# One two-column size matmul, one layer-1 score partial, staged sums and paired weight-block instructions in a TensorE-bound transformer kernel

## The chip, the cores and the metric

The kernel runs on one core of one Trainium2 chip. The metric is the device time of one execution in microseconds (us). Most executions of one kernel agree within 0.3%. "PE" is TensorE, "DVE" VectorE, "ACT" ScalarE, "POOL" GpSimd, "SPq" the queue from which most transfers are issued.

## The reference

Two identical layers work on x of 2048 tokens by 1024, with the same weights in both layers:

```python
def _A_ref(x, wqkv, wo):                 # H = 32 heads of 32; each token sees W = 8 keys, 2 apart
    qkv = (x @ wqkv) ...                 # cut: split into q, k, v and heads
    logits = einsum("bhsd,bhswd->bhsw", q, kg) * Dh ** -0.5   # kg: the 8 gathered keys
    attn = softmax(where(mask, logits, -1e9))
    return einsum("bhsw,bhswd->bhsd", attn, vg) ... @ wo

def _B_ref(x, w1, w3, w2):               # F = 3584
    return (silu(x @ w1) * (x @ w3)) @ w2

x = x + _A_ref(_layernorm(x), wqkv, wo)
x = x + _B_ref(_layernorm(x), w1, w3, w2)
x = x + _A_ref(_layernorm(x), wqkv, wo)
x = x + _B_ref(_layernorm(x), w1, w3, w2)
```

## The kernel before

The tokens are worked in units of 512: four units in layer 0, four in layer 1. In the first two units the gate, up and w2 matmuls are done plainly. While they run, the kernel prepares the same weights for a seven-product (Strassen-Winograd) multiplication, which the other six units use. Preparing a group of weights is a chain across engines:

1. ScalarE squares and sums the group; one small matmul against ones adds the sums over partitions (the "size"); VectorE turns the size into a power-of-two scale.
2. ScalarE copies the four corners of the group, scaled, into a block buffer; VectorE makes the three other blocks as differences; GpSimd issues the stores to DRAM (`t_d`). There are two block buffers, so copies wait for earlier stores.
3. The w2 blocks are made in the same two buffers, after those of w1 and w3. Only when ScalarE has copied w2 is its weight buffer released, and the K and V weights of layer 1 are loaded into released buffers. The second half of the Q weights takes a buffer that the last w3 copies release (in the kernel before it is issued at 495.3, when they end).

The parts that matter here:

```python
def pe_requests(limit=1, must=False):      # small matmuls asked for by the other engines
    act_background()
    while pe_queue and limit and (must or pe_queue[0][0]() + 3.5 <= now["pe"]):
        pe_queue.pop(0)[1]()
        limit -= 1

def act_background():                      # ScalarE's optional work
    for queue in (acts, sizes, parts, reads):
        while True:
            s = head(queue)
            if s is None or max(now["act"], s[1]) + s[0] > now["pe"] + 2.2:
                break
            take_act(queue)

def weight_size(m, g, w, at, got):
    ...                                    # cut: two Square activations into size[:, m, g, 0:2]
    def scale_item(ps, r):
        def emit():
            scale_of(ps[:], up, down)
            got["at"] = now["dve"] + 0.1
        yield 0.8, r, emit
    def add_up(t):
        ps = side.tile([P, 1], FP32, name="size", tag="sd")
        for i in range(2):
            nc.tensor.matmul(ps[:], lhsT=ones[:], rhs=size[:, m, g, i:i + 1], start=i == 0, stop=i == 1)
        makes.append([scale_item(ps, pe(2, t)), None])
    t = now["act"] + 2.5
    pe_queue.append((lambda: t, lambda: add_up(t)))

def weight_sums(m, g, w, got):
    ...                                    # cut: waits for the size and for a free buffer
        for i, (kh, fh) in ((0, (0, 0)), (1, (0, 1)), (3, (1, 0)), (5, (1, 1))):
            yield 0.61, max(got["at"], stored[a]), lambda: nc.scalar.activation(
                b[:, i], w[:, kh * KQ:(kh + 1) * KQ, c0:c0 + P], ACTF.Copy,
                scale=up_scale[:, m, g:g + 1])
        makes.append([differences(m, g, a, now["act"] + 0.1), None])

def differences(m, g, a, r):
    for out, x, y in ((4, 5, 1), (1, 1, 0), (2, 5, 1), (6, 3, 2)):
        yield 0.46, r, lambda: nc.vector.tensor_tensor(b[:, out], b[:, x], b[:, y], op=ALU.subtract)
    ...                                    # cut: two GpSimd stores to t_d
```

A pattern runs through all of it. Every instruction is emitted by a list scheduler written in Python. `now` holds a modelled clock for each engine; each `yield` tells the scheduler a duration (0.61, 0.46, 0.8 ...), the time at which the input is ready, and what to emit. The gate `now["pe"] + 2.2` and the `+ 3.5` decide, by these modelled clocks, whether an instruction goes in here or later. The engines execute in the emitted order.

The activation sums for the seven products (`norm_sums`) are four VectorE instructions, which wait for the transposed activations. The attention scores of one half are products on VectorE, folded down to two partials in `psm`; eight matmuls (`gather_heads`) add these over the head dimension.

Of the kernel before, what the change touches and what calls it, by code (L numbers as in the profile page):

```python
# [17 lines left out]
def kernel(  # L18
# [136 lines left out]

    def bank(name):
        if name == "po":
            return side.tile([P, 512], FP32, name=name, tag="sd")
        return psum.tile([P, 512], FP32, name=name, tag="mm")
# [48 lines left out]
    size2 = const.tile([P, 16], FP32, name="size2")  # L208
    total = const.tile([P, 1], FP32, name="total")
# [4 lines left out]
    h16 = hT[:].bitcast(FP16)  # L214
    t2_d = [dram.tile([P, 7, (b - a) // 2, 512], FP16, name=f"t2_d{i}") for i, (a, b) in enumerate(fsplits)]
    t_d = [[dram.tile([P, 14, KT // 2, P], FP16, name=f"t_d{m}_{g}") for g in range(NG)] for m in range(2)]
    qkv_d = [[dram.tile([P, KT, S], BF16, name=f"qkv_d{l}_{i}") for i in range(3)] for l in range(2)]
# [56 lines left out]
    sums_of, sums_free = {}, [False]  # L274

    def norm_sums(key):

        while not sums_free[0]:
            yield "blocked"
        sums_free[0] = False  # L280
        xnT = xnTs[key]
        KQ = KT // 2
        a11, a12, a21, a22 = [xnT[:, k0:k0 + KQ, t0:t0 + HT] for t0 in (0, HT) for k0 in (0, KQ)]
        s1, s2, s4 = sums[:, 0], sums[:, 1], sums[:, 2]

        def step(out, x, y, op):
            return 0.62, xnT_at[key], lambda: nc.vector.tensor_tensor(out, x, y, op=op)

        yield step(s1, a21, a22, ALU.add)
        yield step(s2, s1, a11, ALU.subtract)  # L290
        yield step(a21, a11, a21, ALU.subtract)
        yield step(s4, a12, s2, ALU.subtract)
        sums_of[key] = now["dve"] + 0.1
# [60 lines left out]

    def act_background():
        for queue in (acts, sizes, parts, reads):
            while True:
                s = head(queue)
                if s is None or max(now["act"], s[1]) + s[0] > now["pe"] + 2.2:
                    break  # L360
                take_act(queue)
# [206 lines left out]
    def score_steps():  # L568

        V = nc.vector  # L570
        for g, (l, h) in enumerate(halves):
# [13 lines left out]
            yield from tree(W, tree_bufs[0], mul_qk, lambda w_: psm[:, w_], True)  # L585
# [5 lines left out]
            def gather_heads(t):  # L591
                at["L"] = L = side.tile([P, W, BLK], FP32, name="L", tag="sd")
                for i in range(2):
                    for a in range(4):
                        nc.tensor.matmul(L[32 * a:32 * (a + 1), :, :], lhsT=gather[:],
                                         rhs=psm[:, :, i, a * BLK:(a + 1) * BLK], start=i == 0, stop=i == 1,
                                         skip_group_check=True)
                at["t"] = pe(3, t) + 0.2
# [71 lines left out]
    for u in range(len(units)):  # L670
        for f0, f1 in fsplits:
# [9 lines left out]
            if u >= TU:  # L681
                seq += [("t2", fsplits.index((f0, f1)), b, nq) for b in range(7)]
# [91 lines left out]

    def sum_later(key):
# [28 lines left out]
    def q_part(l, c, which, ws, then=()):  # L804
# [8 lines left out]
        for t0 in range(0, KT, SG):  # L813
# [19 lines left out]
            if l == 0:  # L833
                stored[:] = landed, landed
# [5 lines left out]
        qkv_at[l, c, which] = landed  # L840
        if which == 2:
# [12 lines left out]
    def weight_size(m, g, w, at, got):  # L854
# [8 lines left out]
        def scale_item(ps, r):  # L863
            def emit():
                scale_of(ps[:], up, down)
                got["at"] = now["dve"] + 0.1
            yield 0.8, r, emit

        def add_up(t):
            ps = side.tile([P, 1], FP32, name="size", tag="sd")  # L870
            for i in range(2):
                nc.tensor.matmul(ps[:], lhsT=ones[:], rhs=size[:, m, g, i:i + 1], start=i == 0, stop=i == 1)
            makes.append([scale_item(ps, pe(2, t)), None])
# [4 lines left out]
    def weight_sums(m, g, w, got):  # L878
# [4 lines left out]
        for a in range(2):  # L883
# [4 lines left out]
            for i, (kh, fh) in ((0, (0, 0)), (1, (0, 1)), (3, (1, 0)), (5, (1, 1))):  # L888
                c0 = fh * 256 + a * P
                yield 0.61, max(got["at"], stored[a]), lambda: nc.scalar.activation(  # L890
                    b[:, i], w[:, kh * KQ:(kh + 1) * KQ, c0:c0 + P], ACTF.Copy,
                    scale=up_scale[:, m, g:g + 1])
            makes.append([differences(m, g, a, now["act"] + 0.1), None])
        made.add((m, g))

    pending, stored, made, held = [0, 0], [0.0, 0.0], set(), []
    junk = hsum[:].bitcast(BF16).rearrange("p k t -> p (k t)")

    def differences(m, g, a, r):

        b = blocks[a]
        for out, x, y in ((4, 5, 1), (1, 1, 0), (2, 5, 1), (6, 3, 2)):
            yield 0.46, r, lambda: nc.vector.tensor_tensor(b[:, out], b[:, x], b[:, y], op=ALU.subtract)
        pending[a] -= 1
        nc.gpsimd.dma_start(t_d[m][g][:, 4 * a:4 * (a + 1)], b[:, 0:4])
        nc.gpsimd.dma_start(t_d[m][g][:, 8 + 3 * a:8 + 3 * (a + 1)], b[:, 4:7])
        stored[a] = now["dve"] + 7.0
# [24 lines left out]
    def measure2(i, n, at):  # L932

        w = hT[:, 0:n, :]
        for a, b in ((0, n // 2), (n // 2, n)):
            def square():
# [3 lines left out]
                if len(measured) == 16:  # L940
                    scales2()
# [15 lines left out]
    def scales2():  # L957

        def scale_item(ps, r):
            def emit():  # L960
                nc.vector.tensor_reduce(total[:], ps[:], op=ALU.add, axis=AX.X)
                scale_of(total[:], up2[:], down2[:])
                got2["at"] = now["dve"] + 0.1
            yield 1.1, r, emit

        def add_up(t):
            ps = side.tile([P, 16], FP32, name="size", tag="sd")
            nc.tensor.matmul(ps[:], lhsT=ones[:], rhs=size2[:], start=True, stop=True)
            makes.append([scale_item(ps, pe(1, t)), None])
# [6 lines left out]
    def sums_of_w2(i, f, ws, loaded):  # L976
# [6 lines left out]
        for j, (fh, hh) in ((0, (0, 0)), (2, (0, 1)), (1, (1, 0)), (5, (1, 1))):  # L983
# [4 lines left out]
        def rest():  # L988
            for out, x, y in ((4, 5, 2), (2, 2, 0), (3, 5, 2), (6, 1, 3)):
                yield 0.46, r, lambda: nc.vector.tensor_tensor(b[:, out], b[:, x], b[:, y], op=ALU.subtract)  # L990
# [17 lines left out]

    def products(u, f0, f1, hold):

        key = ("B", *units[u])
        xnT = xnTs[key]
        KQ = KT // 2
        sides = dict(P1=(0, xnT[:, 0:KQ, 0:HT]), P5=(1, sums[:, 0]), P6=(2, sums[:, 1]), P2=(3, xnT[:, KQ:KT, 0:HT]),
                     P7=(0, xnT[:, 0:KQ, HT:CH]), P3=(1, sums[:, 2]), P4=(2, xnT[:, KQ:KT, HT:CH]))
        groups = [dict(m=m, g=g0 // FG, f=g0 - f0) for g0 in range(f0, f1, FG) for m in range(2)]
# [97 lines left out]
        def acc():  # L1114
            return psum.tile([P, 2, HT], FP32, name="st", tag="mm")

        def run(G, name, out, start, ready=0.0):
            blk, rhs = sides[name]
            w = G["early"] if name in ("P1", "P5", "P6", "P2") else G["late"]
            for a in range(2):  # L1120
                for k in range(KQ):
                    nc.tensor.matmul(out[:, a, :], lhsT=w[:, a, blk, k, :], rhs=rhs[:, k, :],  # L1122
                                     start=start and a == 0 and k == 0, stop=k == KQ - 1, skip_group_check=True)
            return pe(4.05, max(ready, sums_of[key]))

        def consume(G, q, src, r):
            m, g, f = G["m"], G["g"], G["f"] + 2 * (q % 2)
            inv = down_scale[:, m, g:g + 1]
# [14 lines left out]
        def head_part(i, name):  # L1143
            G = groups[i]
            s5, su, s22 = snaps[i % 2], snaps[2], snaps[3]
            if name == "P1":
                G["early"] = weight("early")
                G["A"] = acc()
                r = run(G, name, G["A"], True)
                G["B"] = acc()  # L1150
                nc.scalar.copy(G["B"][:], G["A"][:])  # L1151
                G["tB"] = act(0.5, r)
            elif name == "P5":
                G["D"] = acc()
                r = run(G, name, G["D"], True)
                nc.scalar.activation(s5, G["D"][:], ACTF.Copy, scale=down_scale[:, G["m"], G["g"]:G["g"] + 1] if G["m"] else 1.0)
                G["t5"] = act(0.5, r)
            elif name == "P6":
                r = run(G, name, G["A"], False, G["tB"])
                nc.scalar.copy(su, G["A"][:])  # L1160
                G["tU"] = t = act(0.5, r)
                background(t + 0.8)
                nc.vector.tensor_tensor(G["D"][:], G["D"][:], su, op=ALU.add)  # L1163
                G["tD"] = dve(0.68, max(t, G["t5"])) + 0.1
            elif name == "P2":
                r = run(G, name, G["B"], False, G["tB"])
                release(1)
                consume(G, 0, G["B"][:], r)
            elif name == "P7":
                G["late"] = weight("late")  # L1170
                r = run(G, name, G["A"], False, G["tU"])
                background(r + 0.8)
                if G["m"]:
                    s22 = tight[:, 0]
                    nc.vector.scalar_tensor_tensor(s22, G["A"][:], down_scale[:, 1, G["g"]:G["g"] + 1], s5,
                                                   op0=ALU.mult, op1=ALU.add)
                else:
                    nc.vector.tensor_tensor(s22, G["A"][:], s5, op=ALU.add)  # L1178
                G["tC"] = dve(0.68, r) + 0.1
                consume(G, 3, s22, G["tC"])  # L1180
            elif name == "P3":
# [194 lines left out]
```

## Time and profile before

| | before |
|---|---|
| time, median of 3 (lowest to highest) | 1545.78 us (1545.72 to 1547.3) |
| span of the profiled execution | 1546.5 us |
| PE / DVE / ACT busy | 1529.9 / 1191.9 / 883.3 us |
| mean granted clock | 0.997 |

Two lines of the page of the kernel before, the span and the busy times of the engines with their share of the span:

```profile
span 1546.5 us, 25176 instructions
...
PE 1529.9 (99%) x9694; PEld 992.7 (64%) x9694; DVE 1191.9 (77%) x2048; ACT 883.3 (57%) x1388; POOL 158.8 (10%) x308
```

TensorE bounds the kernel: 1529.9 of 1546.5 us. But the share is of no use for judging what is left to gain. The Trainium skill ("Perfetto Trace Analysis", Identifying the Most-Contended Engine) says that the busy share of matmuls is a poor measure of headroom. A matmul at half clock counts as busy too (2.00 of 2.00 us at a clock of 0.50 in a stretch shown below). The lines to read are the waits and the granted clock.

The next lines are the largest of TensorE's waits in the kernel before: what waited, for which engine and line, the total in us, how many times, and the longest.

```profile
PE L L595 <- DVE psm L506: 4.1, 1, 4.1
PE w L1057 <- DVE hT L1028: 2.6, 3, 1.4
PE w L1057 <- ACT big L1077: 1.9, 4, 0.6
...
PE po L762 <- DVE x_sb L767: 0.9, 1, 0.9
```

The first is a single wait. The timeline of VectorE before that place shows its cause. The columns are start and length in us, then the instructions; in brackets stand the idle time before them and what ended it.

```profile
530.91 1.23 DVE L582 TENSOR_TENSOR tree<-qT,kT 128x2048 bf16<-128x2048 bf16 x1
542.21 0.69 DVE L287 TENSOR_TENSOR big<-xnT 128x1024 f16<-128x1024 f16 x1 [10.08 <-DMA xnT<-xn]
542.82 0.42 DVE L506 TENSOR_TENSOR psm<-tree 128x512 bf16<-128x512 bf16 x1
543.16 0.68 DVE L287 TENSOR_TENSOR big<-big,xnT 128x1024 f16<-128x1024 f16 x1
...
544.96 0.68 DVE L502 TENSOR_TENSOR tree<-tree 128x1024 bf16<-128x1024 bf16 x1
545.68 0.42 DVE L506 TENSOR_TENSOR psm<-tree 128x512 bf16<-128x512 bf16 x1
```

VectorE works in order. Activation sums (L287) had been put ahead of the folds (L502, L506), and the first waited 10.08 us for the transposed activations. So the last fold ended at 546.1. The timeline of TensorE:

```profile
537.83 4.26 PE L820 MATMUL ps<-xnT,wqkv 128*128 128x512 f16 x19
546.16 1.05 PE L595 MATMUL L<-psm,gather 128*32 128x512 bf16 x8 [4.06 <-DVE psm L506]
```

The gather waits 4.06 us for that fold. The windows view of the kernel before then shows the price in clock (length of the stretch; busy time and count of PE, PEld, DVE, ACT and POOL; granted clock; DMA share; GB/s):

```profile
546.00:548.00 2.00, 1.84 (x10) 0.52 (x10) 0.82 (x3) 0.00 (x0) 0.00 (x0) 0.50 1.01 418
...
550.00:552.00 2.00, 2.00 (x6) 0.82 (x5) 1.29 (x2) 1.22 (x3) 0.00 (x0) 0.50 1.16 313
```

The clock is 0.50 in these two stretches; the half clock runs from 545.2 to 552.0, 6.8 us. TensorE works in it only from 546.2 on, 5.8 us, of which half, 2.9 us, is lost. The stall costs 4.06 + 2.9 = 7.0 us. The Trainium skill ("TensorE: Matmul & The Clock Gate", Part 1: The HAM clock gate) has the half clock follow an idle window of about 3.4 us; this place agrees roughly, with 4.06 us idle, the clock halved 3.1 us after the wait began (542.1), and a stretch twice 3.4 us long.

The groups that the change rewrites, from the views of the kernel before by line and shape (count, busy us, mean ns, then idle time before):

```profile
L890 ACT ACTIVATE big<-w1t,up_scale 128x512 f16<-128x512 bf16 x56 | 36.1, 711 | 9.2 <-DVE psm L506 5.1 <-DMA t_d<-big 4.1
...
L903 DVE TENSOR_TENSOR big<-big 128x512 f16<-128x512 f16 x112 | 47.2, 423 | 15.9 <-ACT big L890 13.7
...
L595 PE MATMUL L<-psm,gather 128*32 128x512 bf16 x128 | 10.3, 399 | 4.1 <-DVE psm L506 4.1
...
L872 PE MATMUL size<-size,ones 128*128 128x1 f32 x56 | 7.0, 229 | 0.0
```

### The profile page before, as it was taken

To read this page: it belongs to the slowest core of one execution; us is meant where nothing else is said; L and a number is where in the kernel's file an instruction comes from. 1 tells how busy PE (TensorE), PEld (TensorE's weight loads), DVE (VectorE), ACT (ScalarE), POOL (GpSimd) and SP (SyncE) were. 2 spreads that over 40 slices of the span, in tenths; PEclk is the share of its full clock that TensorE was granted. 3 is DMA by queue.
4 is the path that set the end of the run, shared out by engine and by line. 5 is a ranking of instruction groups with operands and counts; after the bars stand their busy time and mean duration, and the time that the engine had idled before them with its cause. 6 is when DMAs were issued, how large, how long until landed. Compare 5 with 4: busy or idle time off the path is not lost.

```text
span 1546.5 us, 25176 instructions
## 1 busy us (share of the span) xinstructions
PE 1529.9 (99%) x9694; PEld 992.7 (64%) x9694; DVE 1191.9 (77%) x2048; ACT 883.3 (57%) x1388; POOL 158.8 (10%) x308
## 2 busy tenths in 40 slices
PE   9999999999999989999999999999999999999999
PEld 7666644444444568675685766866677667686866
DVE  4788988889889688989798958798668977435345
ACT  4885466657565346555574564756557446554633
POOL 1210102111111000101001020100101001000000
PEclk9999999999999999999999999999999999999999
DMA  9777969798898798979979888797979988878885
GB/s 330 202 222 203 265 222 319 255 305 284 249 329 290 241 307 316 316 265 295 296 269 339 309 261 284 277 318 275 334 249 316 339 296 276 303 275 327 311 292 207
DMA packets 261432, 439.57 MB, mean 284 GB/s; under 512 B 73856, under 2 KB 201088, under 8 KB 245056
## 3 DMA queue, kind: packets, MB, share of 16 engines
q1 hardware_dynamic: 248464, 390.90, 76.6%
q0 software_dynamic: 12704, 46.93, 8.2%
q8 instruction: 76, 1.25, 0.3%
q14 instruction: 44, 0.36, 0.1%
q10 hardware_dynamic: 144, 0.13, 0.0%
HBM read 345.90 MB, written 67.90 MB: 268 GB/s over the span
## 4 chain that ended last, share of the span: by engine, by line
PE 83%; DVE 9%; ACT 3%; DMA 3%; issue 1%; POOL 1%; SPq 1%; ACTq 0%; DVEq 0%; POOLq 0%
PE st L1122 28%; PE ps L820 18%; PE w L1057 11%; PE po L762 7%; PE pg L1243 6%; PE acc L1274 6%; PE pu L1252 6%; DVE tree L656 1%; DMA wqkv<-in_A_wqkv_dram 1%; DVE tree L502 1%; PE pq L436 1%; DVE tree L582 1%; DVE hT L1028 1%; DMA xnT<-xn 1%; DVE hT L1140 1%
## 5 line engine op out<-in xcount | busy, mean ns | idle before, releaser
L820 PE MATMUL ps<-xnT,wqkv 128*128 128x512 f16 (+1 forms) x1472 | 323.3, 381 | 0.3 <-DMA wqkv<-in_A_wqkv_dram 0.2
L1122 PEld LDWEIGHTS <-early 128*128 128x128 f16 x2688 | 262.8, 98 | 38.2 <-issue 1.4
L820 PEld LDWEIGHTS <-wqkv 128*128 128x128 bf16 x1472 | 210.7, 144 | 111.8 <-issue 5.8
L1057 PE MATMUL w<-t,hT 128*128 128x512 f16 x1008 | 226.4, 379 | 4.6 <-DVE hT L1028 2.6
L1122 PEld LDWEIGHTS <-late 128*128 128x128 f16 x2016 | 197.0, 98 | 31.2 <-issue 3.2
L582 DVE TENSOR_TENSOR tree<-qT,kT 128x2048 bf16<-128x2048 bf16 x128 | 156.3, 1221 | 30.0 <-ACT big L824 14.8
L502 DVE TENSOR_TENSOR tree<-tree 128x1024 bf16<-128x1024 bf16 x256 | 175.1, 684 | 0.9
L1122 PE MATMUL st<-xnT,late 128*128 128x256 f16 x1344 | 174.2, 273 | 1.0 <-DVE big L1178 0.7
L1057 PEld LDWEIGHTS <-hT 128*128 128x128 f16 x1008 | 98.0, 98 | 118.5 <-DVE hT L1028 5.4
L1122 PE MATMUL st<-big,early 128*128 128x256 f16 x1344 | 172.2, 273 | 0.2
L1122 PE MATMUL st<-xnT,early 128*128 128x256 f16 x1344 | 165.7, 273 | 0.0
L656 DVE TENSOR_TENSOR tree<-At,vT 128x2048 bf16<-128x2048 bf16 x128 | 156.2, 1220 | 7.9 <-DMA At<-E 6.5
L1151 ACT COPY st<-st 128x512 f32<-128x512 f32 x84 | 48.4, 576 | 125.1 <-PE st L1122 124.3
L762 PE MATMUL po<-wo,oT 128*128 128x512 bf16 x512 | 115.9, 379 | 0.9 <-DVE x_sb L767 0.9
L1252 PE MATMUL pu<-xnT,w3t 128*128 128x512 f16 x448 | 105.8, 379 | 0.0
L1243 PE MATMUL pg<-xnT,w1t 128*128 128x512 f16 x448 | 105.8, 379 | 0.0
L824 ACT CAST hT<-ps 128x512 bf16<-128x512 f32 x96 | 55.6, 585 | 81.5 <-PE ps L820 80.3
L1163 DVE TENSOR_TENSOR st<-st,big 128x512 f32<-128x512 f32 x84 | 58.4, 695 | 51.9 <-ACT big L1160 51.8
L1274 PE MATMUL acc<-w2t,hT 128*128 128x512 bf16 x448 | 98.2, 379 | 0.0
L1131 ACT ACTIVATE sg<-st,down_scale 128x512 bf16<-128x512 f32 x126 | 86.5, 687 | 11.5 <-PE st L1122 10.9
L1122 PE MATMUL st<-big,late 128*128 128x256 f16 x672 | 87.1, 273 | 0.0
L762 PEld LDWEIGHTS <-oT 128*128 128x128 bf16 x512 | 50.1, 98 | 56.8 <-issue 1.2
(166 smaller groups left out, 1912.0 us busy)
## 6 DMA issues: line engine op xcount, KB each, us to landing
early<-t_d SPq DMA_DIRECT2D x84, 1024.0 KB, 6.5
late<-t_d SPq DMA_DIRECT2D x84, 768.0 KB, 6.4
t<-t_d SPq DMA_DIRECT2D x42, 1024.0 KB, 7.1
t<-t_d SPq DMA_DIRECT2D x42, 768.0 KB, 5.3
wqkv<-in_A_wqkv_dram SPq DMA_DIRECT2D x28, 1024.0 KB, 8.2
w1t<-in_B_w_dram SPq DMA_DIRECT2D x14, 1024.0 KB, 9.3
w3t<-in_B_w_dram SPq DMA_DIRECT2D x14, 1024.0 KB, 11.5
t_d<-big POOLq DMA_DIRECT2D x28, 512.0 KB, 7.1
```

The costliest lines, as they stand in the source:

```text
L502: nc.vector.tensor_tensor(b, b, buf[:, 4:8, :], op=ALU.add)
L582: V.tensor_tensor(pr, qT[:], kT[:, :, k0:k0 + TCH], op=ALU.mult)
L656: V.tensor_tensor(tm.rearrange("p w (a e) -> p w a e", a=4), At[:].rearrange("p a w e -> p w a e"), win, op=ALU.mult)
L762: nc.tensor.matmul(ps[:], lhsT=oT[:, t, j * P:(j + 1) * P], rhs=wo[:, t, hh * 512:(hh + 1) * 512], start=(t == 0), stop=(t == KT - 1))
L820: nc.tensor.matmul(ps[:], lhsT=ws[kk // KH][:, kk % KH, t::KT], rhs=xnT[:, kk, :], start=(kk == 0), stop=(kk == KT - 1))
L1057: nc.tensor.matmul(out[:], lhsT=lhs[:, k, j * P:(j + 1) * P], rhs=w[:, k, :], start=start and k == 0, stop=k == nq - 1, skip_group_check=True)
L1122: nc.tensor.matmul(out[:, a, :], lhsT=w[:, a, blk, k, :], rhs=rhs[:, k, :], start=start and a == 0 and k == 0, stop=k == KQ - 1, skip_grou ...
L1131: nc.scalar.activation(sg[:], src, ACTF.Silu, scale=inv)
L1163: nc.vector.tensor_tensor(G["D"][:], G["D"][:], su, op=ALU.add)
L1243: nc.tensor.matmul(pg[:], lhsT=w1t[:, kk, fi * P:(fi + 1) * P], rhs=xnT[:, kk, :], start=(kk == 0), stop=(kk == KT - 1))
L1252: nc.tensor.matmul(pu[:], lhsT=w3t[:, kk, fi * P:(fi + 1) * P], rhs=xnT[:, kk, :], start=(kk == 0), stop=(kk == KT - 1))
L1274: nc.tensor.matmul(acc[:], lhsT=hT[:, f, j * P:(j + 1) * P], rhs=tiles[hh][f // nq][:, f % nq, :], start=(f == 0), stop=(f == f1 - f0 - 1))
```

## The change

It means to take work from three engines: one size matmul instead of two; four score-gather matmuls instead of eight in layer 1, for one more fold on VectorE; two block copies, and two of the differences, as one instruction each; and activation sums that wait one by one, just before the product that needs them. The core of the diff:

```diff
+    opened = [0]
+    def side_tile(*args, **kw):            # a PSUM tile of the side pool
+        while opened[0]:                   # an unread size is read first
+            take(makes)
+        return side.tile(*args, **kw)
...
-            ps = side.tile([P, 1], FP32, name="size", tag="sd")
-            for i in range(2):
-                nc.tensor.matmul(ps[:], lhsT=ones[:], rhs=size[:, m, g, i:i + 1], start=i == 0, stop=i == 1)
-            makes.append([scale_item(ps, pe(2, t)), None])
+            ps = side_tile([P, 2], FP32, name="size", tag="sd")
+            opened[0] += 1
+            nc.tensor.matmul(ps[:], lhsT=ones[:], rhs=size[:, m, g, :], start=True, stop=True)
+            makes.insert(0, [scale_item(ps, pe(1, t)), None])       # scale_item: a reduction more
...
-            for i, (kh, fh) in ((0, (0, 0)), (1, (0, 1)), (3, (1, 0)), (5, (1, 1))):
-                yield 0.61, max(got["at"], stored[a]), lambda: nc.scalar.activation(
-                    b[:, i], w[:, kh * KQ:(kh + 1) * KQ, c0:c0 + P], ACTF.Copy,
+            for i, j, fh in ((0, 2, 0), (3, 6, 1)):
+                yield 1.20, max(got["at"], stored[a]), lambda: nc.scalar.activation(
+                    b[:, i:j + 1:j - i], w[:, :, c0:c0 + P].rearrange("p (h k) c -> p h k c", h=2), ACTF.Copy,
...
-        for out, x, y in ((4, 5, 1), (1, 1, 0), (2, 5, 1), (6, 3, 2)):
-            yield 0.46, r, lambda: nc.vector.tensor_tensor(b[:, out], b[:, x], b[:, y], op=ALU.subtract)
+        yield 0.66, lambda: tt(b[:, 1:5:3], b[:, 3:7:3], b[:, 0:4:3], op=ALU.subtract)
+        yield 0.42, lambda: tt(b[:, 3], b[:, 4], b[:, 0], op=ALU.add)
+        yield 0.42, lambda: tt(b[:, 5], b[:, 2], b[:, 3], op=ALU.subtract)
...
+            parts_ = 2 if l == 0 else 1                              # layer 1: one partial
-                for i in range(2):
+                for i in range(parts_):
                     for a in range(4):
                         nc.tensor.matmul(L[32 * a:32 * (a + 1), :, :], lhsT=gather[:],
...                                          # norm_sums: each sum waits for its own slot,
...                                          # and is forced before P5, P6, P3 or P7 only
```

The rest of the diff is a rewrite of the product pipeline as a function of its own, the block order that the new layout needs, and code that is defined and never called. The copies of w2 remain single.

## The prediction

> **What bounds the kernel.** TensorE: the busy table gives it 1529.9 of 1546.5 us (VectorE 77%, ScalarE 57%). Its matmuls already stream: in the chain of waits 216 projection matmuls take 46.78 us (217 ns each), 320 gate/up products 34.93 us (109 ns each). Only fewer passes or fewer stalls save time. The list of TensorE waits has about 12 us. One place stands out: at 542.1 us TensorE waits 4.06 us for the first layer-1 score gather. In the timeline VectorE has the activation sums (L287) queued ahead of the last two score folds; they wait 10.1 us for transposed activations that land at 542. Then the windows view has a mean granted clock of 0.66 over 542 to 552 us, and 49 matmuls take 13.15 us where 49 x 0.216 = 10.6 would do. The Trainium skill ("TensorE: Matmul & The Clock Gate", Part 1, the HAM clock gate) says an idle window of about 3.4 us halves the clock; this stall of 4.06 us agrees. That place costs about 7 us.
>
> **What the change does.** The V products are defined but never called; the gate constant keeps its value.
> - Size, TensorE: 28 fp32 one-column matmuls (56 passes) become 14 of two columns (28 passes). A pair takes 0.37 us in the timeline, one (the w2 size) 0.14 to 0.19: saves 0.2 x 14 = 3 us.
> - Gather, TensorE: layer 1 uses 4 matmuls, not 8, per half; 8 take 0.55 us: estimate 0.27 x 8 = 2 us.
> - Block copies, ScalarE: 112 of 711 ns become 56 of an estimated 1.24 us (a 1024-element scaled activation took 1241 ns): -10 us.
> - Differences, VectorE: 168 of 423 ns become 84 of 423 and 42 of about 684: -7 us. Size reductions: +2 us.
> - Layer 1's extra fold, VectorE: 64 x 285 ns = +18 us.
>
> ScalarE and VectorE figures are off the critical path; they count only where TensorE waits for them.
>
> **What it moves.** The built order matters most. The last layer-0 output-projection tiles stand earlier on TensorE (84 w2 matmuls follow the last, 12 before), so the norm and its four transposes come earlier. The score gather stands after 24 projection matmuls, not 112, and its folds before the sums. The wait and the half clock should vanish: -7 us. Against this, the last w3 size now stands 12 matmuls into the w2 stage, so the last block copies, w2 copies and the release of the w2 buffers come later; the K weights load into those buffers and already cost 0.5 us at 532. I expect 3 us back there. In layer 1 the folds meet a VectorE that is 80 to 90% busy from 550 to 1080 us: 1 us of new waits. Staged sums remove a forced wait that shows no idle time: 0.
>
> **Sum.** -3 -2 -7 +3 +1 = -8: **1538 us**, range 1531 to 1545. Faster by over 2%: 2%; within 2%: 97%; slower by over 2%: 1%.
>
> **What would show it.** Right: 28 size passes, 96 gathers; no TensorE wait over 3 us near 542 and no half clock after the start; TensorE busy about 1522, VectorE 1206, ScalarE 873. Wrong: a wait of 3 us or more at the K projection for its weights or for ScalarE (clock halved again), or rising TensorE waits on VectorE in the w2 products (L1057 before, 4.6 us).
>
> **What would make it wrong.** The stall reappearing in full (about 1544); the added folds pushing attention behind the output projection; or the scheduler's chance order opening a new clock drop.

## The result, and the profile after

| | before | after |
|---|---|---|
| time, median of 4 (lowest to highest) | 1546.04 us (1545.72 to 1547.3) | 1550.51 us (1546.14 to 1551.54) |
| ratio, 95% interval | | 1.0022 (1.0002 to 1.0042) |
| span of the profiled execution | 1546.5 us | 1549.2 us |
| PE / DVE / ACT busy | 1529.9 / 1191.9 / 883.3 us | 1524.6 / 1199.0 / 874.0 us |
| TensorE idle in the span | 16.6 us | 24.6 us |

The trace after has 9594 matmul records for 9634 weight loads, the trace before 9694 for 9694: 40 records are missing, and the small gaps that they leave count as idle. The idle time that stands as waits of TensorE rose from 12.5 to 18.7 us.

The prediction was 1538 with a range of 1531 to 1545; the result lies above the range. The page of the kernel after:

```profile
span 1549.2 us, 24956 instructions
...
PE 1524.6 (98%) x9594; PEld 990.4 (64%) x9634; DVE 1199.0 (77%) x2084; ACT 874.0 (56%) x1332; POOL 158.8 (10%) x308
```

The rewritten groups, after:

```profile
L915 ACT ACTIVATE big<-w1t,up_scale 128x1024 f16<-128x1024 bf16 x28 | 30.8, 1138 | 7.2 <-DVE up_scale L875 6.4 <-DVE big L927 0.8
...
L927 DVE TENSOR_TENSOR big<-big 128x1024 f16<-128x1024 f16 x42 | 28.9, 688 | 27.3 <-ACT big L1049 23.4 <-ACT big L915 3.8
...
L609 PE MATMUL L<-psm,gather 128*32 128x512 bf16 x96 | 8.1, 386 | 0.0
...
L897 PE MATMUL size<-size,ones 128*128 128x2 f32 x28 | 3.9, 209 | 0.0
```

The work itself came out as costed. A double copy takes 1138 ns where two took 2 x 711, a double difference 688 ns where two took 2 x 423; the size matmuls take 3.9 us, not 7.0, the gathers 8.1, not 10.3. What went up is idle time. TensorE's waits in the kernel after:

```profile
PE po L776 <- DVE down_scale L889: 4.5, 3, 2.5
PE ps L841 <- ACT hT L845: 2.3, 1, 2.3
PE ps L841 <- DMA wqkv<-in_A_wqkv_dram: 2.3, 1, 2.3
PE st L1091 <- ACT big L1112: 2.2, 1, 2.2
PE pg L1354 <- ACT sg L1358: 1.6, 1, 1.6
PE st L1091 <- ACT sg L1302: 1.4, 1, 1.4
...
PE st L1091 <- ACT st L1103: 1.2, 2, 0.8
```

The one wait of 4.1 us has gone. Seven lines stand in its place that were absent, or 0.2 us, before, and two of them are at the first projection of layer 1, seen here in TensorE's timeline:

```profile
520.43 1.03 PE L841 MATMUL ps<-xnT,wqkv 128*128 128x512 f16 x4
523.77 6.22 PE L841 MATMUL ps<-xnT,wqkv 128*128 128x512 f16 x20 [2.31 <-DMA wqkv<-in_A_wqkv_dram]
529.92 0.62 PE L609 MATMUL L<-psm,gather 128*32 128x512 bf16 x8
530.47 5.40 PE L841 MATMUL ps<-xnT,wqkv 128*128 128x512 f16 x24
538.20 3.02 PE L841 MATMUL ps<-xnT,wqkv 128*128 128x512 f16 x8 [2.33 <-ACT hT L845]
```

The prediction and the expectations call this place the K projection. Counted in the trace it is the projection of Q: the three projections of a unit have 64 matmuls each, Q first, and the two waits stand before the 5th and the 49th. K begins at 543.1 and does not wait for its weights. So TensorE waits 2.31 us for the second half of the Q weights, and 2.33 us for the cast (L845) that frees a PSUM bank.

The first wait comes from the order of the DMA queue. Its timeline in the kernel after:

```profile
508.16 1.27 SPq L277 DMA_TRANSPOSE xnT<-xn  x1
509.48 2.01 SPq L712 DMA_DIRECT2D wqkv<-in_A_wqkv_dram  x2
```

and in a_split, a run told below with the same instructions in another order:

```profile
489.54 2.98 SPq L712 DMA_DIRECT2D wqkv<-in_A_wqkv_dram  x2
```

In the kernel after the Q weights stand behind a transposition of activations, for which the queue waited 13.1 us, until 508.1, on VectorE's `xn`; they go out at once after it. In a_split they stand before it. For the second wait ScalarE's timeline of the kernel after shows why:

```profile
501.35 4.27 ACT L915 ACTIVATE big<-w3t,up_scale 128x1024 f16<-128x1024 bf16 x4 [5.12 <-issue]
523.83 1.95 ACT L1049 ACTIVATE big<-w2t,up 128x512 f16<-128x512 bf16 x3 [18.22 <-DMA t_d<-big]
...
535.12 2.56 ACT L1049 ACTIVATE big<-w2t,up 128x512 f16<-128x512 bf16 x4 [5.73 <-DMA t_d<-big]
537.58 2.99 ACT L845 CAST hT<-ps 128x512 bf16<-128x512 f32 x6
```

The last block copies of w3 (L915) run at 501.35. The copies of w2 (L1049) need the same two buffers, wait 18.22 us for the stores of blocks (`t_d<-big`), and are followed by another 5.73 us wait. The casts of the Q projection stand behind them in ScalarE's order and start at 537.58. The K and V weights hang on the same copies and are issued from 535.9 to 538.3, but TensorE does not wait for them. Nor can these copies have delayed the Q weights, which were there when the first of them began. Two stretches of the windows view of the kernel after:

```profile
526.00:528.00 2.00, 2.00 (x6) 0.78 (x5) 1.00 (x2) 1.79 (x3) 0.00 (x0) 0.50 1.00 223
...
540.00:542.00 2.00, 2.00 (x6) 0.81 (x5) 1.93 (x5) 1.16 (x3) 0.73 (x1) 0.50 1.05 403
```

The clock is 0.50 in both. In all, this kernel has half clock from 525.1 to 528.5, from 538.8 to 542.2 and from 1006.4 to 1009.8, each 3.4 us, of which 1.7 us is lost.

The ledger of the two profiled executions, worked out from these views:

| term | predicted us | read us | from |
|---|---|---|---|
| size matmuls | -3 | -3.1 | groups, 7.0 to 3.9 |
| score gathers | -2 | -2.2 | groups, 10.3 to 8.1 |
| stall at 542 and its half clock gone | -7 | -7.0 | 4.06 + 2.9 |
| first projection of layer 1 (Q; predicted as K) | +3 | +8.0 | waits 2.31 + 2.33, two half-clock stretches 2 x 1.7 |
| output projection waits for the size read (L889) | not foreseen | +3.6 | 4.5, less 0.9 that it waited before |
| gate matmuls of the second unit (461) | not foreseen | +1.6 | waits |
| layer 1 | +1 | +1.9 | waits 2.2 + 1.4 + 1.2 and 1.7 for half clock, less 2.6 + 1.1 + 0.9 that went |
| sum | -8 | +2.8 | spans differ by +2.7 |

In the layer-1 row the 1.1 is the fall of the w2 products' wait for ScalarE from 1.9 to 0.8, and the 0.9 two waits for VectorE of 0.7 and 0.2 that the kernel after does not have. A ledger from one profiled execution of each kernel is an account, not a proof. The experiments are there for that. What is read are differences of about 1% and less, by their intervals.

### The profile page after: what moved, and what is told of

It is laid out like the page before. It is cut to its first block, busy times and chain, and to the rows that moved or that the text cites. A ratio compares the mean times of both kernels' runs of the same rounds, so it can differ in the third digit from the quotient of the medians.

```text
span 1549.2 us, 24956 instructions
## 1 busy us (share of the span) xinstructions
PE 1524.6 (98%) x9594; PEld 990.4 (64%) x9634; DVE 1199.0 (77%) x2084; ACT 874.0 (56%) x1332; POOL 158.8 (10%) x308
## 4 chain that ended last, share of the span: by engine, by line
PE 62%; ACT 3%; DMA 1%; DVE 1%; issue 1%; ACTq 0%
PE st L1091 31%; PE w L1240 16%; PE ps L841 10%; PE po L776 4%; DMA t_d<-big 1%; ACT L634 0%; ACT L1302 0%; ACT big L1049 0%; ACT sg L1302 0%; ACT E L634 0%; PE L L609 0%; DVE hT L1211 0%; ACT st L1103 0%; DVE tree L595 0%; DVE x_sb L1225 0%
## 5 line engine op out<-in xcount | busy, mean ns | idle before, releaser
L670 DVE TENSOR_TENSOR tree<-At,vT 128x2048 bf16<-128x2048 bf16 x128 | 156.1, 1220 | 12.5 <-DMA At<-E 11.3
L776 PE MATMUL po<-wo,oT 128*128 128x512 bf16 x486 | 111.3, 379 | 5.9 <-DVE down_scale L889 4.5
L845 ACT CAST hT<-ps 128x512 bf16<-128x512 f32 x96 | 55.4, 586 | 77.2 <-PE ps L841 73.8
## 6 DMA issues: line engine op xcount, KB each, us to landing
t_d<-big POOLq DMA_DIRECT2D x28, 512.0 KB, 6.9
```

The lines of the kernel that those rows point to most:

```text
L670: V.tensor_tensor(tm.rearrange("p w (a e) -> p w a e", a=4), At[:].rearrange("p a w e -> p w a e"), win, op=ALU.mult)
L776: nc.tensor.matmul(ps[:], lhsT=oT[:, t, j * P:(j + 1) * P], rhs=wo[:, t, hh * 512:(hh + 1) * 512], start=(t == 0), stop=(t == KT - 1))
```

## The experiments

Theory A is that the order of the instructions, not the work, costs the time: in the new order the size of the last w3 group comes late, and with it the chain copies, differences, stores, w2 copies, release, load of the K weights (the two waits read above are on the Q weights and on a cast, so only part of this chain can be what TensorE waited for). The rivals are that an instruction of the change costs more than was thought (longer copies that block ScalarE, folds that fill VectorE), or, at the end, that the new waits merely replace each other. "The order of before" means that the edit gives the scheduler the durations of the kernel before, so the sequence of that kernel stays. The edits are shown shortened. Each batch ran on one chip with the kernel before, whose median was 1546.87, 1546.88, 1547.17 and 1547.34 us in the four batches.

### First batch: work against order

**w_all**: all work changes, put into the order of before. The first step of each pair is told and emits nothing; the added fold is emitted without a told duration of its own.

```diff
-   yield 0.61, ..., copy one block       # four times
+   yield 0.61, ..., nothing              # then, at the second's place:
+   yield 0.61, ..., copy two blocks
    ...                                   # differences likewise; one size matmul; one partial
```

> The kernel before, its order kept: one two-column size matmul, one layer-1 partial and the fused copies and differences are put in, but the scheduler is told the old costs, so every other instruction stands where it stood. Theory A (the work saved is real, the loss comes from the order): TensorE busy falls by 5 us, the wait of 4 us at 542 and its half clock stay, time about 1541 us (ratio 0.997). Rival B (the removed passes were not worth their 5 us, or the added folds eat it): 1545 us or more.

Measured: 1547.0 us, ratio 0.9998 (0.9983 to 1.0013). The 1541 that theory A asked for was missed. The stall stayed (4.3 us, half clock 6.8 us), as it had to in this order. The trace is some 3 us ahead of the kernel before until 1012 us and loses this again in layer 1 by 1090 us, where the waits on hT (2.8 us, 2.6 before), ScalarE (2.6, 1.9 before) and the Q weights of the last unit (1.4, 0.2 before) have grown. These increases do not make up the whole 3 us. So the work alone is not worth 5 us in an order that was made for other work, and theory A is only half of the story.

**a_append**: the kernel after, with the size read put at the end of VectorE's queue, as before, and not forced.

```diff
-   makes.insert(0, [scale_item(ps, pe(1, t)), None])
+   makes.append([scale_item(ps, pe(1, t)), None])
-   while opened[0]: take(makes)
```

> The changed kernel, but the size's reduction goes to the back of VectorE's queue again and is not forced when a PSUM side tile is opened. The size matmuls of the built order return to about their old places (the last w3 size stands before the w2 stage). Theory A (the late last size delays block copies, w2 copies and K weights): the ScalarE wait of 18 us for the stores shrinks to about 9, the two waits of 2.3 us at 523 and 538 and the 4.5 us of waits for the size read go; time 1541 to 1545 us. Rival C (the extra folds on VectorE in layer 1 are the loss): stays at 1548 to 1551.

Measured: 1541.69 us, ratio 0.9965 (0.9948 to 0.9982). The stalls at the Q projection and the waits of the output projection for the size read are gone. One new wait of 5.4 us stands at 567.7, with 3.4 us of half clock.

**a_uncopy**: the kernel after, with four single copies told 0.61 each.

```diff
-   for i, j, fh in ((0, 2, 0), (3, 6, 1)):            yield 1.20 ... two blocks
+   for i, (kh, fh) in ((0, (0, 0)), (2, (1, 0)), (3, (0, 1)), (6, (1, 1))):  yield 0.61 ... one block
```

> The changed kernel with the ScalarE block copies separate again (four of half the size, at the old cost for the scheduler). The built order has the early sizes again. Theory A: no wait above 1 us at the K projection, time 1539 to 1544 although ScalarE is 9 us busier. Rival D (any order of the changed kernel is as slow, the loss lies in layer 1): 1548 to 1551.

Measured: 1536.17 us, ratio 0.9926 (0.9911 to 0.9941). ScalarE works 884.2 us, more than after, and there is no wait over 1.6 us. Either the double copy is bad in itself, or its told duration of 1.20 is.

**a_twopart**: the kernel after, with two partials in layer 1.

```diff
-   parts_ = 2 if l == 0 else 1
+   parts_ = 2
```

> The changed kernel with two layer-1 partials as before. Its order up to the first layer-1 stage is the same as the changed kernel's, so the stalls before 545 us stay. Theory A: those stalls and their half clocks remain, time 1548 to 1552, 2 us of passes more, VectorE 18 us less busy. Rival C (folds): the layer-1 waits on ScalarE (1.4, 0.8, 2.2 us) go and the time falls to 1545 or less.

Measured: 1552.78 us, ratio 1.0038 (1.0019 to 1.0056). The waits before 545 us stay (2.45 us at 526.4, 2.15 at 540.7, 2.53 at 288). The single partial is not what costs. Up to 625 us every engine has the order of the kernel after, and yet here the wait of 2.53 us at 288 is followed by 3.4 us of half clock (from 288.7), while in the kernel after the same wait is followed by none. So a clock drop can come in one execution and stay away in another, and it moves 1.7 us here.

### Second batch: the double copy, the late size, the parts alone

**a_split**: the kernel after, instruction for instruction; only the scheduler is told two steps of 0.61 for one double copy.

```diff
-   yield 1.20, max(got["at"], stored[a]), lambda: nc.scalar.activation(   # two blocks
+   yield 0.61, max(got["at"], stored[a]), lambda: None
+   yield 0.61, max(got["at"], stored[a]), lambda: nc.scalar.activation(   # two blocks
```

> The changed kernel, instruction for instruction (same kinds and counts on every engine), but the scheduler is told that a fused block copy is two steps of 0.61 us, of which only the second issues it, instead of one step of 1.20 us. On TensorE, VectorE, GpSimd and the DMA queue the built order is then identical to that of the run with separate copies. Theory A (order alone made the loss): 1534 to 1538 us, no wait above 2 us on TensorE and no half clock after the start. Rival E (the fused instructions themselves are slow or come late for their users): 1541 us or more while the separate copies had 1536.

Measured: 1536.22 us, ratio 0.9933 (0.9919 to 0.9948). This run decides between work and order. The program has the same instructions as the kernel after, double copies included, and its PE, DVE, POOL and SP orders are those of a_uncopy. It is 14 us faster than the kernel after. Its largest TensorE waits:

```profile
PE st L1092 <- ACT big L1113: 3.1, 5, 1.0
PE pu L1364 <- DMA w3t<-in_B_w_dram: 1.6, 1, 1.6
```

TensorE at the first projection of layer 1 in a_split:

```profile
518.76 16.35 PE L841 MATMUL ps<-xnT,wqkv 128*128 128x512 f16 x75
535.04 0.62 PE L609 MATMUL L<-psm,gather 128*32 128x512 bf16 x8
```

75 matmuls run without a gap where the kernel after stops twice. ScalarE at the same place:

```profile
503.41 5.01 ACT L1050 ACTIVATE big<-w2t,up 128x512 f16<-128x512 bf16 x8 [11.28 <-DMA t_d<-big]
516.08 2.56 ACT L1050 ACTIVATE big<-w2t,up 128x512 f16<-128x512 bf16 x4 [7.67 <-DMA t_d<-big]
518.55 0.56 ACT L845 CAST hT<-ps 128x512 bf16<-128x512 f32 x1
```

The w2 copies start at 503.41, not 523.83, and the casts at 518.55, not 537.58. In a_split the last size matmul stands at 477.2; in the kernel after it stands at 498.7.

**a_late**: a_split, in which only the last w3 size is asked for 20 us later.

```diff
-   t = now["act"] + 2.5
+   t = now["act"] + (2.5 if (m, g) != (1, NG - 1) else 22.5)
```

> The same as the split-step kernel, but the last w3 size matmul alone is asked for 20 us later in the schedule, so that it stands 36 matmuls into the w2 stage. Theory A (the late size delays block copies, stores, w2 copies and so the K weights): waits of more than 2 us at the Q and K projection come back, with at least one half-clock stretch; 6 to 15 us slower than the split-step kernel. Rival F (the size's place does not matter): within 2 us of it.

Measured: 1552.53 us, ratio 1.0037 (1.0022 to 1.0052). A stall at the first projection of layer 1 is back:

```profile
521.78 4.48 PE L841 MATMUL ps<-xnT,wqkv 128*128 128x512 f16 x20
535.85 4.50 PE L841 MATMUL ps<-xnT,wqkv 128*128 128x512 f16 x12 [9.58 <-ACT hT L845]
```

ScalarE in a_late:

```profile
503.98 4.27 ACT L916 ACTIVATE big<-w3t,up_scale 128x1024 f16<-128x1024 bf16 x4 [17.49 <-DVE up_scale L875]
523.59 5.01 ACT L1050 ACTIVATE big<-w2t,up 128x512 f16<-128x512 bf16 x8 [15.35 <-DMA t_d<-big]
532.77 2.56 ACT L1050 ACTIVATE big<-w2t,up 128x512 f16<-128x512 bf16 x4 [4.17 <-DMA t_d<-big]
535.23 2.99 ACT L845 CAST hT<-ps 128x512 bf16<-128x512 f32 x6
```

The size matmul stands at 502.7; ScalarE waits for it (`up_scale`) with its w3 copies, which start at 503.98; the w2 copies follow at 523.59 and the casts at 535.23. TensorE waits 9.58 us, and the clock is halved for 10.2 us, most of it during the wait: 3.6 us of work run at half clock. The wait is on the cast, the second of the two in the kernel after; TensorE waits neither for Q nor for K weights here. One late size is thus enough to bring the stall on the cast. It does not bring the other one, and that it is the whole cause in the kernel after does not follow.

**w_size**: the order of before, with one two-column size matmul and the reduction.

```diff
-   for i in range(2): nc.tensor.matmul(ps[:], lhsT=ones[:], rhs=size[:, m, g, i:i + 1], ...)
+   nc.tensor.matmul(ps[:], lhsT=ones[:], rhs=size[:, m, g, :], start=True, stop=True)
```

> The kernel before, order kept, only the two size matmuls made one of two columns. If its 14 removed matmuls are worth what the trace showed: 3 us less TensorE time up to 480 us and 1542.5 to 1545 us. If other waits take it back: 1546 to 1547.

Measured: 1544.66 us, ratio 0.9989 (0.9972 to 1.0006); by medians 2.2 us less than the kernel before. The interval touches 1, so the sign is likely and not certain.

**w_gather**: the order of before, with one partial in layer 1. The added fold is emitted without a told duration.

```diff
-   yield from tree(W, tree_bufs[0], mul_qk, lambda w_: psm[:, w_], True)
+   yield from tree(W, tree_bufs[0], mul_qk, lambda w_: psm[:, w_, 0:parts_], True, l == 1)
```

> The kernel before, order kept, only layer 1's one partial: 32 gather matmuls fewer, 64 folds more on VectorE. If the passes are worth 2 us and the folds are hidden: about 1544 to 1545. Rival (the 18 us of folds delay what TensorE waits for in layer 1, which took back the gain of the all-parts run between 1000 and 1090 us): 1546.5 us or more, with waits on VectorE and on the weights of the last projection up by 2 us or more.

Measured: 1549.22 us, ratio 1.0017 (1.0002 to 1.0032). VectorE works 1209 us. The gathers saved on TensorE (2.2 us) were outweighed: its waits grew from 12.5 to 16.4 us, by about 2 us each on VectorE and on ScalarE. That VectorE fell behind the scheduler's clock, which had not been told of the folds, is a likely reading and not shown. The stall at 546 (3.98 us) is followed by 3.4 us of half clock here, not 6.8.

### Third batch: what the parts are worth in which order

**a_gate**: the kernel after, with ScalarE's gate at 2.8 us, so that the built order has the last size early again.

```diff
-   gate[0] = 2.2
+   gate[0] = 2.8
```

> The changed kernel with one constant changed: the scheduler lets a ScalarE background step end up to 2.8 us after TensorE's time instead of 2.2. Same instructions; the last w3 size again stands before the w2 stage, the output projections early in it. Theory A (order alone): waits at the Q and K projection below 2 us in all, no half clock there, 1535 to 1541 us. Rival G (only the particular order of the split-step kernel is good, the constant does not reach the cause): 1546 or more.

Measured: 1548.92 us, ratio 1.0012 (0.9995 to 1.0028). The number of theory A was missed. Waits of 0.88 us for Q weights and 1.22 us for K weights are left, without a half clock; but at 491 to 494 the w2 matmuls now wait 1.47 and 2.21 us for VectorE and 6.8 us run at half clock, and a product waits 4.6 us at 577.7. Mending one stall by moving the order opened two others.

**a_split_two**: a_split with two partials in layer 1.

```diff
-   parts_ = 2 if l == 0 else 1
+   parts_ = 2
```

> The split-step kernel with two layer-1 partials again: the same order up to the first layer-1 stage. If one partial is worth its 32 gather matmuls when the scheduler knows of the folds: 1 to 3 us slower than the split-step kernel, so 1537 to 1539. If the 18 us of folds cost as much as in the run with before's order (2.3 us lost): 1534 to 1535.

Measured: 1542.32 us, ratio 0.9968 (0.9953 to 0.9983). Against a_split the single partial is worth 6 us where its fold is told. In the two profiles 1.7 us of this are gather matmuls (9.9 against 8.1) and 1.6 us waits of TensorE (11.1 against 9.5; 2.8 us of them of the w2 products on hT, which a_split does not have); the rest is not traced to a cause. In w_gather, untold, it cost 2.3 us.

**w_fuse**: the order of before, with double copies and differences alone.

```diff
-   four copies and four differences for a block buffer
+   two double copies, one double and two single differences, at the places of before
```

> The kernel before, order kept, only the copies and differences fused. ScalarE 10 us and VectorE 7 us less busy, TensorE the same. If neither is on the critical path: within 1 us of before, 1546 to 1547.5, with the 4 us wait at 542 and its half clock unchanged. Rival: the shorter chain of copies and stores brings the K weights earlier: 1544 or less.

Measured: 1546.58 us, ratio 0.9996 (0.9981 to 1.0011). ScalarE works 874.4 us and VectorE 1187.2, 9 and 5 us less than before, and the time does not move; the stall at 546 (4.4 us) is unchanged. Neither engine bounds the kernel.

**b_fuse**: the kernel before with the double instructions; a double copy is told as 1.20, while the differences keep their four steps of 0.46.

```diff
-   yield 0.61 (x4), four copies
+   yield 1.20 (x2), two double copies    # differences: 0.46 (x4) as before, the first emits nothing
```

> The kernel before with only the copies and differences fused, and the scheduler told the new costs (1.20 us for one copy). Theory A: this alone moves sizes and output projections; in the built order the second w1 size group stands in the w2 stage and the last output projections stand within the Q projection, so the norm before the first layer-1 stage comes late and TensorE waits over 3 us for the activation sums at about 545 us with a half clock: 1548 to 1556. Rival H (the told cost of the fused copy is harmless by itself, it needs the forced reading of the size): 1546 or less.

Measured: 1547.29 us, ratio 1.0000 (0.9985 to 1.0015). The new duration reorders this kernel too: the stall at 542 is gone, and the output projection now waits 5.0 us for VectorE (longest 2.7, with a half clock of 3.4 us). The told 1.20 alone does not give the stalls of the kernel after; it does so together with the forced size read.

### Fourth batch: is the late size the whole cause?

**a_early**: the kernel after, with the last w3 size asked for 8 us earlier.

```diff
-   t = now["act"] + 2.5
+   t = now["act"] + (2.5 if (m, g) != (1, NG - 1) else -5.5)
```

> The changed kernel with one thing moved: the last w3 size matmul is asked for 8 us earlier, so that it stands directly behind the one before it, ahead of the w2 stage. TensorE's order is otherwise the same. Theory A: the ScalarE wait of 18 us for the stores shrinks, the waits of 2.3 us at 523 and at 538 and the two half clocks there shrink to under 2 us in all; 5 to 8 us faster than the changed kernel: 1542 to 1546. The waits of TensorE for the size read (2.5 and 1.8 us at 287 and 405) stay. Rival I (the stalls of the K projection have another cause): still 1549 to 1551.

Measured: 1548.36 us, ratio 1.0009 (0.9994 to 1.0024). The size matmul stands at 483.6 now, 15 us earlier, right behind the two squares that it adds up (they end at 483.5). But the block copies are spread out to 503.2, ScalarE reaches the w2 copies only at 522.2, after a wait of 16.9 us for stores, and TensorE waits 3.4 us for the casts at 536.5, with 6.8 us of half clock. The Q weights still stand behind the transposition and go out at 511.3 and 512.0, in time for a projection that itself begins at 521.6. So in the kernel after the late last size is not the sole cause; what comes before and behind it is late as well. GpSimd's timeline tells the same: the last six stores ahead of the w2 copies are issued from 484.7 to 498.2 in a_split, and from 498.8 to 516.8 in the kernel after; in a_early the last of them is issued at 517.5. Earlier ones lag a_split too, in the kernel after and in a_early alike: the store that a_split issues at 282.3 is issued at 299.9 and 299.5. The lag is not carried on unchanged: the store of 372.8 in a_split comes at 378.7 and 377.3.

**a_mm**: the kernel after in identical order, with the size result in one of the other PSUM banks, so that the output projection need not wait for the size read.

```diff
-   ps = side_tile([P, 2], FP32, name="size", tag="sd")
+   while opened[0]: take(makes) if head(makes) is not None else None
+   ps = psum.tile([P, 2], FP32, name="size", tag="mm")
```

> The changed kernel, same built order on every engine, but the size result lies in one of the six other PSUM banks and not in one of the two side banks, so that an output projection need not wait until VectorE has read the size. Theory A': the 4.5 us of waits for the size read go and nothing takes their place: 1545 to 1547. Rival J (those waits only move, to the six banks or to the next operand): 1549 to 1551.

Measured: 1552.58 us, ratio 1.0035 (1.0019 to 1.0052). The 4.5 us of waits for the size read are gone and nothing is gained: the output projection waits 2.2 us for another instruction of VectorE at 288, the up matmuls 4.3 us for ScalarE at 459, and 6.8 us run at half clock. These waits only moved.

**a_early_mm**: both edits.

```diff
    the edits of a_early and a_mm together
```

> Both at once, order as in the early-size run. If the two causes add up: 9 to 12 us faster than the changed kernel, 1538 to 1542. What is then left against the split-step kernel's 1536 are the ScalarE waits in the first layer-1 stages. Rival: the gains overlap, 1543 or more.

Measured: 1550.61 us with single runs of 1543.82, 1553.23, 1549.15 and 1552.07; ratio 1.0013 (0.9989 to 1.0038). Inconclusive: one and the same program spread over 9 us. The kernel after has such a spread too (1546.14 to 1551.54). The mean clocks of the four runs differ (0.999, 0.998, 0.998, 0.995), but do not order the times: the slowest run has 0.998, and 0.001 of clock is 1.5 us of 1546. In the kernel after, runs of 1551.54 and 1546.14 both have 0.999. So clock drops explain a part of the spread at most.

### All runs

| kernel | median us | ratio (95%) | what it is |
|---|---|---|---|
| after | 1550.51 | 1.0022 (1.0002 to 1.0042) | the change |
| w_all | 1547.0 | 0.9998 (0.9983 to 1.0013) | all work, old order |
| w_size | 1544.66 | 0.9989 (0.9972 to 1.0006) | size, old order |
| w_gather | 1549.22 | 1.0017 (1.0002 to 1.0032) | one partial, old order, fold untold |
| w_fuse | 1546.58 | 0.9996 (0.9981 to 1.0011) | double instructions, old order |
| b_fuse | 1547.29 | 1.0000 (0.9985 to 1.0015) | double instructions, double copy told as 1.20 |
| a_append | 1541.69 | 0.9965 (0.9948 to 0.9982) | after, size read not forced |
| a_uncopy | 1536.17 | 0.9926 (0.9911 to 0.9941) | after, single copies |
| a_split | 1536.22 | 0.9933 (0.9919 to 0.9948) | after, same instructions, told as two |
| a_split_two | 1542.32 | 0.9968 (0.9953 to 0.9983) | a_split, two partials |
| a_late | 1552.53 | 1.0037 (1.0022 to 1.0052) | a_split, one size late |
| a_twopart | 1552.78 | 1.0038 (1.0019 to 1.0056) | after, two partials |
| a_gate | 1548.92 | 1.0012 (0.9995 to 1.0028) | after, another gate |
| a_early | 1548.36 | 1.0009 (0.9994 to 1.0024) | after, last size early |
| a_mm | 1552.58 | 1.0035 (1.0019 to 1.0052) | after, size in another bank |
| a_early_mm | 1550.61 | 1.0013 (0.9989 to 1.0038) | both |

## Why the prediction was right or wrong

- **Size, -3 us: right.** The groups read -3.1, and w_size, alone in the old order, -2.2 us by medians.
- **Gathers, -2 us: right for the passes, too small for the whole.** The passes fell by 2.2 us. What the single partial is worth differs with the order: +2.3 us in the old order with the fold untold (w_gather), -6 us told in the order of a_split (against a_split_two), -2.3 us told in the order of the kernel after (against a_twopart, 1.7 us of it the half clock at 288). That the telling decides this is likely and not shown, since the orders differ too.
- **Double copies and differences off the critical path: right.** Busy times were predicted as 1206 for VectorE and 873 for ScalarE, and read as 1199.0 (a rise of 7 us, not 14) and 874.0; w_fuse shows that they move no time by themselves. TensorE's busy time was predicted as 1522 and read as 1524.6, though 40 matmul records are missing from that trace; new half-clock stretches add to it: a_split, with the same instructions and a mean clock of 1.000, has 1520.5. The double copy was thought to take 1.24 us and takes 1.14.
- **The stall at 542 gone, -7 us: right.** Neither it nor its half clock is in the trace after.
- **"I expect 3 us back there": this step failed, in its path and in its size.** The prediction had the last w3 size come late, and with it the block copies, the w2 copies, the release of their buffers and the K weights, for which TensorE would wait 3 us. The runs show the late copies, but TensorE never waits for K weights in the kernel after. It waits 2.31 us for Q weights that stand behind a transposition in the DMA queue, and 2.33 us for a cast that stands behind the w2 copies on ScalarE; two half-clock stretches cost 3.4 us more. Together this is 8.0 us, not 3. The prediction had counted waiting time, and named the halved clock, and a wait for ScalarE, only as signs by which to know it wrong. a_late shows that a late size is enough to produce the stall on the cast. But one size is not the whole cause: a_early, which puts it 15 us earlier, gains only 2 us, within the spread of single runs, because the stores were late without it.
- **"1 us of new waits" in layer 1: direction right, size low.** By the ledger +1.9 us net, with a clock drop at 1006 that was not foreseen.
- **Missing altogether: 3.6 us of waits for the forced size reads and 1.6 us at 461.** The forced read was given no cost. a_mm shows that removing this wait alone gives nothing, so it is not a cost that can be taken off on its own.
- **"Staged sums ... 0": not tested alone.** No run here undoes them.
- **"The scheduler's chance order opening a new clock drop"** was the last item under what would make it wrong. It is what happened: three half-clock stretches, two of them at the place where 3 us were expected.

The strongest finding is a_split. It has the instructions of the kernel after, one told duration aside, and takes 1536.2 us. The gains predicted for the change (-3 -2 -7) were therefore there to be had; the first three terms of the ledger make -12.3 us, and the spans differ by 12.7 (1533.8 against 1546.5). The closeness is partly luck, since other small waits differ between the two as well. In the kernel as changed, the order gave all of them back. Two decisions made it together, so far as the runs go: a double copy told as one step of 1.20, and a size read put first and forced. Undoing either (a_split, a_append) removes the stalls at the Q projection.

What stays open: which single placement earlier in layer 0 makes the chain of stores late (by 18 us at the store that a_split issues at 282, by 6 us at that of 373, by 19 us at the last one), which one puts the Q weights behind the transposition, and why single runs of one program differ by up to 9 us. a_gate and a_mm each mended a place and opened another, and a_early left the stall on the cast.

The version to keep is a_split: 1536.2 us, ahead of both kernels.

## What to carry to other kernels

Where a scheduler with told durations places the instructions, a change of duration is a change of order: put the new work into the old order, and the old step lengths around the new work, before judging the work. Cost a stall on the bounding engine as its wait plus half of the work that then runs at half clock, and look for the half clock even after waits near 2 us. Follow a late item through the buffers and the queues that it shares, and count which operand the stalled instruction reads: here a late copy held back the casts behind it, and a transposition held back the weights behind it.

## What the Trainium skill lacked or had wrong

- "TensorE: Matmul & The Clock Gate", Part 1 and "Why this matters for your kernels": the page gives a free-running window of 3413 ns and advises against gaps over about 3 us. The stretches at half clock here agree with the window (3.4, 6.8 and 10.2 us), but shorter waits preceded them: 2.31 us at 523.8, 2.33 us at 538.2 and 2.2 us at 1006.3 in the kernel after, 1.47 and 2.21 us at 491 to 494 in a_gate. A wait of 2.53 us at 288 in the kernel after was followed by none, and the same wait in a_twopart, in the same order, by 3.4 us. Gaps under 3 us are thus not safe, and the length of the wait alone does not decide.
- The same page, Part 1, calls the number of cold matmuls run-variable at the start of a kernel. It does not say that clock drops in the middle of a tuned kernel are run-variable too: the stall near 545 (3.98 us in w_gather, 4.21 us in w_size) is followed by 3.4 us of half clock in one and goes with 6.8 us in the other, and the wait at 288 by 3.4 us or none.
- "Perfetto Trace Analysis", Optimizing Scalar/DVE Operations: it gives an overhead of about 93 ns for an instruction of ScalarE and 60 ns for one of VectorE on SBUF, about twice that in a profiled duration. Merging two into one saved 2 x 711 - 1138 = 284 ns of profiled duration on ScalarE and 2 x 423 - 688 = 158 ns on VectorE here, more than twice the figures. In busy time w_fuse saved 8.9 us for 56 merged pairs on ScalarE, 159 ns each, and 4.7 us for 42 on VectorE, 112 ns each, against 93 and 60. Its remark that grouping helps if the engine is saturated agrees: with ScalarE at 57%, w_fuse gained nothing (0.9996).
- No page has it that durations told to a scheduler inside the kernel decide the time of a program with the same instructions: 1550.5 us against 1536.2 us here.
